# Attention kernel: a hand-made head, a searched instruction order and a 45th key block on VectorE

## The chip, the cores and the metric

The kernel runs on one core of a Trainium2 chip. The time is what the device needs for one execution, in microseconds (us); smaller is better. A single core has no second die to be compared with, so a run counts as fast here unless it is over 1.5% above the fastest one of its kernel. "Span" is the time from the first to the last record in a profile; it is about 1.8 us shorter than the time of the same execution. "Faster" or "slower" is said from 2% on.

## The reference

It is a gated mix of a full 16-head softmax attention and a spectral filter over 2048 positions of 448 features (head size 28), all inputs in bfloat16. Cut to what matters:

```python
def reference(A_x, A_wqkv, A_wo, B_x, B_w_r, B_w_i, gate_w):
    # B, S, D, H = 1, 2048, 448, 16
    g = sigmoid((A_x * gate_w).sum(-1, keepdims=True))
    q, k, v = split(A_x @ A_wqkv)                  # 16 heads of 28
    p = softmax(einsum("bhqd,bhkd->bhqk", q, k) * 28 ** -0.5)
    a = merge(einsum("bhqk,bhkd->bhqd", p, v)) @ A_wo
    b = irfft2(rfft2(B_x) * (B_w_r + 1j * B_w_i))  # ... cut
    return g * a + (1 - g) * b
```

The 2048 x 2048 scores of 16 heads need 67 million exponentials. They are the bulk of the work.

## The kernel before

Queries are handled in 16 groups (four heads times 512 queries), keys in 16 blocks of 128. A block of a group is four units of 128 x 512 scores. ScalarE takes units three at a time from the PSUM tile `psA` and two at a time from `psB`, in alternation, and writes the exponentials into a ring of 28 slots, from which TensorE multiplies them with the values. `ND` says how many key blocks of each group go to VectorE instead, which approximates the exponential by integer arithmetic on the bits in four phases:

```python
    ND = [1, 2, 3, 3, 2, 3, 3, 3, 3, 3, 3, 3, 3, 3, 3, 3]   # 44 of 256 blocks on VectorE
    # ... cut
            # ScalarE: one step of the row of exponentials
            def fe(st=st, slot=slot, u0=u0):
                self.pin(nc.scalar.activation(out=self.ring[:, u0:u0 + len(st), :], in_=slot[:, 0:len(st), :],
                                              func=ACT.Exp, scale=LN2 / UNITS))
    # ... cut
                # VectorE: from PSUM (four times for a block), then one of four phases in SBUF
                def f1(s=s, it=it, ys=ys):
                    self.pin(nc.vector.tensor_scalar(out=ys[:, s, :], in0=self.bgi(it), scalar1=127 * UNITS,
                                                     scalar2=0.0, op0=ALU.add, op1=ALU.max))
                # ... cut
                def g1(ys=ys, pds=pds, f=f):
                    fl = lambda t: t[:].rearrange("p a b -> p (a b)")
                    self.pin(nc.vector.tensor_scalar(out=fl(pds).bitcast(U16), in0=fl(ys), scalar1=float(PHASE[f]),
                                                     scalar2=0.25, op0=ALU.add, op1=ALU.mult))
```

The head loads weights and the first 512 rows of x, pads the weights, transposes x on TensorE, and computes the first q and k. Fourteen matmuls on zeros ("warm-ups") are there to get TensorE to its fast rate. In the traces here matmuls of 256 columns stand 0.11 us apart at the fast rate and 0.21 at the half rate:

```python
        d1 = [self.dma(free_dims(self.U[:], [[112, 3], [1, 112]], W0 + 336 * i), ...,     # 84 KB of k or q weights
                       eng=eng, dur=0.55, lat=2.9) for i, eng in ((0, "SP"), (1, "AQ"))]
        d2 = self.dma(free_dims(self.U[0:64, 0, :], [[112, 2], [1, 112]], W0 + 672), ..., # 28 KB, 64 rows, q and k
                      eng="AQ", dur=0.55, lat=2.9)
        # ... cut
        self.wready["k", 0] = padcopy("k", 0, raw0("k"), dk, K0 + 3.95, "DVE")
        self.wready["q", 0] = padcopy("q", 0, raw0("q"), dq, K0 + 4.05, "ACT")
        for i in range(14):
            self.pe(256, lambda: self.mm(self.psA[:, 2, 0:256], self.zero[:, 0:P], self.zero[:], True, True),
                    (ms["zero"],), K0 + i * .01, dur=0.214)
```

All 3,123 operations are made first and then emitted in an order that is written out as a list. `FILLS` adds matmuls on zeros at places where TensorE would sit idle, and `BANKS` chooses one of two PSUM banks for each short-lived tile.

```python
        done = set()
        for p, i in enumerate(ORDER):
            while j < len(FILLS) and FILLS[j][0] == p:
                n, t = FILLS[j][1:]
                # ... cut: append a filler matmul of n columns
            o = self.ops[i]
            assert all(d in done for d in o.deps)
            done.add(o)
            order.append(o)
        return order
```

The waits on the chip come from the tiles that the instructions read and write, not from the `deps` of this list; the list only fixes each engine's order.

## Time and profile before

| | before |
|---|---|
| time, median of 3 runs (range) | 411.84 us (410.68 to 412.26) |
| span of the profiled run | 409.6 us |
| head: start to first exponential | 13.72 us |
| row: first exponential's start to the last one's end | 386.81 us |
| tail: from there to the end of the span | 9.07 us |
| exponentials on ScalarE | 340 |

Three rows sum up to the span, and every change must show in one of them. In a line of the page the figures behind the bar are busy time in us and mean ns of one instruction, then the idle time of the engine ahead of the group and what ended most of it. In a timeline the first two columns are start and duration in us; `x4` is four instructions in a row, and the bracket gives the idle time ahead and what ended it. The prediction shows the lines.

### The profile page before, as it was taken

What the parts mean: (1) busy time and instruction counts of PE and PEld (TensorE: products, weight loads), DVE (VectorE), ACT (ScalarE), POOL (GpSimd) and SP (SyncE); (2) the same over time, 40 slices, a digit from 0 to 9 for tenths busy, and PEclk for the clock granted to TensorE, in tenths of its full rate; (3) what the DMA queues carried; (4) which work ended last, traced back from release to release, by engine and by line L of the source; (5) the groups of instructions that cost most, each with busy time, mean ns of one, the idle gap of its engine ahead of it and who ended that gap; (6) DMA issues with size and microseconds to landing.
All of it is one profiled execution on the core that took longest, in us unless ns stands there. A gap on an engine that the chain in (4) does not pass through costs nothing.

```text
span 409.6 us, 12755 instructions
## 1 busy us (share of the span) xinstructions
PE 392.5 (96%) x5469; PEld 152.3 (37%) x5469; DVE 365.9 (89%) x629; ACT 389.8 (95%) x358; POOL 41.9 (10%) x95
## 2 busy tenths in 40 slices
PE   5999999999999999999999999999999999999995
PEld 4644333333543333334333333433334343333333
DVE  2768998889999999999999999999999998988784
ACT  2699999999999999999999999999999999999991
POOL 6121400000040000000040000001400000000000
PEclk9999999999999999999999999999999999999999
DMA  7820000000221221101110010043121110010111
GB/s 200 240 51 5 3 3 2 4 2 4 74 52 46 56 63 43 44 3 47 44 45 3 2 29 21 19 123 107 44 71 55 30 28 14 2 37 2 27 52 63
DMA packets 26548, 18.00 MB, mean 44 GB/s; under 512 B 10704, under 2 KB 24956, under 8 KB 26492
## 3 DMA queue, kind: packets, MB, share of 16 engines
q1 hardware_dynamic: 25660, 16.94, 15.3%
q8 instruction: 42, 0.69, 0.7%
q10 hardware_dynamic: 832, 0.26, 0.3%
q14 instruction: 14, 0.11, 0.1%
HBM read 11.31 MB, written 1.84 MB: 32 GB/s over the span
## 4 chain that ended last, share of the span: by engine, by line
ACT 53%; PE 34%; issue 8%; DVE 2%; POOL 1%; DMA 1%; ACTq 0%; DVEq 0%; POOLq 0%
ACT ring L1286 53%; PE bg L572 14%; PE pvb L572 9%; PE psA L572 6%; PE psB L572 5%; DVE y L1239 1%; DMA CR<-cRB 1%; PE bg L581 0%; POOL wpq L671 0%; POOL vd L875 0%; POOL wo L880 0%; DVE pd L1249 0%; ACT w L1068 0%; ACT t L1498 0%; DVE pvs L1399 0%
## 5 line engine op out<-in xcount | busy, mean ns | idle before, releaser
L1286 ACT ACTIVATE ring<-psA 128x1536 bf16<-128x1536 f32 x170 | 266.1, 1566 | 2.7 <-PE psB L572 1.9
L1286 ACT ACTIVATE ring<-psB 128x1024 bf16<-128x1024 f32 (+1 forms) x170 | 193.2, 1136 | 0.6 <-PE psB L572 0.6
L1239 DVE TENSOR_SCALAR y<-bg 128x512 uint16<-128x512 f32 x176 | 117.8, 683 | 8.2 <-PE bg L572 6.8
L1249 DVE TENSOR_SCALAR pd<-y 128x2048 uint16<-128x2048 uint16 x176 | 117.5, 685 | 0.6
L572 PEld LDWEIGHTS <-k 32*128 32x128 bf16 (+1 forms) x1064 | 44.0, 91 | 116.9 <-issue 110.3
L572 PE MATMUL pvb<-ring,vw 128*32 128x512 bf16 (+1 forms) x872 | 75.4, 377 | 0.3 <-DVE pvs L1399 0.2
L572 PE MATMUL psA<-q,k 32*128 32x512 bf16 (+1 forms) x525 | 68.0, 376 | 5.1 <-ACT ring L1286 2.8
L572 PE MATMUL psB<-q,k 32*128 32x512 bf16 (+1 forms) x347 | 67.8, 378 | 0.8 <-ACT ring L1286 0.5
L572 PE MATMUL bg<-q,k 32*128 32x512 bf16 x176 | 65.7, 380 | 0.8 <-DVE y L1239 0.3
L572 PE MATMUL pvb<-pd,vd 128*32 128x512 bf16 x704 | 63.2, 384 | 0.0
L572 PEld LDWEIGHTS <-vw 128*32 128x32 bf16 x872 | 20.7, 95 | 29.6 <-issue 24.6
L572 PEld LDWEIGHTS <-vd 128*32 128x32 bf16 x704 | 16.7, 94 | 27.6 <-issue 23.8
L1404 POOL CAST rhl<-rr 128x16 bf16<-128x16 f32 x15 | 4.0, 267 | 223.9 <-DVE rr L1403 223.9
L572 PEld LDWEIGHTS <-xT 128*128 128x128 bf16 (+3 forms) x512 | 19.3, 96 | 12.7 <-issue 10.1
L1142 POOL TENSOR_SCALAR vd<-vf 128x348 bf16<-128x348 f32 x16 | 19.5, 1222 | 33.4 <-DVE vf L1131 32.6
L1624 DVE CAST Y<-bg 128x450 bf16<-128x450 f32 x32 | 19.7, 618 | 1.2 <-PE bg L572 0.7
L572 PE MATMUL bg<-xT,wpk 128*32 128x512 bf16 (+2 forms) x244 | 18.3, 381 | 0.0
L572 PE MATMUL bg<-xT,wpq 128*32 128x512 bf16 (+1 forms) x240 | 17.7, 383 | 0.0
L572 PE MATMUL bg<-Bd,xT 128*32 128x450 bf16 (+1 forms) x256 | 17.1, 357 | 0.0
L572 PE MATMUL bg<-wo,q 128*32 128x448 bf16 x236 | 16.7, 355 | 0.0
L572 PE MATMUL bg<-Bd,xtok 113*32 113x448 bf16 x240 | 16.5, 355 | 0.0
L572 PE MATMUL bg<-X,R 128*32 128x225 bf16 (+1 forms) x288 | 14.3, 294 | 0.0
(130 smaller groups left out, 322.6 us busy)
## 6 DMA issues: line engine op xcount, KB each, us to landing
U<-Y SPq DMA_DIRECT2D x32, 112.5 KB
CR<-cRB SPq DMA_DIRECT2D x8, 256.0 KB
out_dram<-U SPq DMA_DIRECT2D x14, 112.0 KB
CR<-cCS SPq DMA_DIRECT2D x8, 192.0 KB
xtok<-in_A_x_dram SPq DMA_DIRECT2D x3, 448.0 KB
xT<-escr SPq DMA_DIRECT2D x2, 512.0 KB
Wg<-in_B_w_r_dram SPq DMA_DIRECT2D x8, 112.5 KB
Wg<-in_B_w_i_dram SPq DMA_DIRECT2D x8, 112.5 KB
```

The lines of the kernel that those rows point to most:

```text
L572: self.pin(self.nc.tensor.matmul(out, lhsT=lhsT, rhs=rhs, start=start, stop=stop, **kw))
L1142: self.pin(nc.gpsimd.tensor_scalar(out=self.vd[g][:, f, :, :, 0:DH + 1], in0=self.vf[:], scalar1=PHGAIN[f], scalar2=None, op0=ALU.mult))
L1239: self.pin(nc.vector.tensor_scalar(out=ys[:, s, :], in0=self.bgi(it), scalar1=127 * UNITS, scalar2=0.0, op0=ALU.add, op1=ALU.max))
L1249: self.pin(nc.vector.tensor_scalar(out=fl(pds).bitcast(U16), in0=fl(ys), scalar1=float(PHASE[f]), scalar2=0.25, op0=ALU.add, op1=ALU.mult))
L1286: self.pin(nc.scalar.activation(out=self.ring[:, u0:u0 + len(st), :], in_=slot[:, 0:len(st), :], func=ACT.Exp, scale=LN2 / UNITS))
L1404: b = self.pool(0.3, lambda: self.pin(nc.gpsimd.tensor_copy(out=rhl[:, 0, :], in_=rr[:])), (a,), kk)
L1624: self.pin(nc.vector.tensor_copy(out=y[:], in_=self.bgi(it)[:, 0:F2]))
```

## The change

The intent is to start the exponentials sooner by a head arranged by hand, to give one more key block to VectorE, and to have everything else ordered by a search. In code it is one number and three lists (and `TA`, which only feeds sort keys that the written-out order overrides):

```diff
@@ class Sched / lists @@
-ORDER = ( 119, 1, 0, 2, 7, 3, 12, 22, 94, 4, 21, 13, 32, 6, ...   # 3,123 numbers, cut
+ORDER = ( 1, 2, 7, 0, 8, 10, 19, 3, 20, 21, 12, 11, 13, 4, ...    # 3,134 numbers, cut
-FILLS = ( (117, 192, 0), (126, 256, 1), (144, 256, 0), ...         # 10,976 columns in all, cut
+FILLS = ( (121, 256, 0), (121, 256, 0), (121, 256, 0), ...         # 12,640 columns in all, cut
-BANKS = ( ... cut
+BANKS = ( ... cut
-TA, TB = 43.678, 14.609
+TA, TB = 36.0, 14.609
@@ class Kernel @@
-    ND = [1, 2, 3, 3, 2, 3, 3, 3, 3, 3, 3, 3, 3, 3, 3, 3]
+    ND = [1, 3, 3, 3, 2, 3, 3, 3, 3, 3, 3, 3, 3, 3, 3, 3]
```

## The prediction

> **What bounds the kernel now.** I read the page first (busy shares, chain, groups), then the timelines of ScalarE, VectorE and TensorE over the first 20 us, the waits, and the busy time by stretches.
>
> ```profile
> PE 392.5 (96%) x5469; PEld 152.3 (37%) x5469; DVE 365.9 (89%) x629; ACT 389.8 (95%) x358; POOL 41.9 (10%) x95
> ...
> ACT 53%; PE 34%; issue 8%; DVE 2%; POOL 1%; DMA 1%; ACTq 0%; DVEq 0%; POOLq 0%
> ...
> L1286 ACT ACTIVATE ring<-psA 128x1536 bf16<-128x1536 f32 x170 | 266.1, 1566 | 2.7 <-PE psB L572 1.9
> L1286 ACT ACTIVATE ring<-psB 128x1024 bf16<-128x1024 f32 (+1 forms) x170 | 193.2, 1136 | 0.6 <-PE psB L572 0.6
> L1239 DVE TENSOR_SCALAR y<-bg 128x512 uint16<-128x512 f32 x176 | 117.8, 683 | 8.2 <-PE bg L572 6.8
> L1249 DVE TENSOR_SCALAR pd<-y 128x2048 uint16<-128x2048 uint16 x176 | 117.5, 685 | 0.6
> ```
>
> Three engines look full, but ScalarE leads: 340 exponentials (170 of three units of 512 columns, 170 of two) wait only 3.3 us together (2.7 + 0.6), and more than half of the chain is that one line. So the end is: start of the first exponential, plus the row of exponentials, plus a tail. The start and the tail:
>
> ```profile
> 4.40 0.66 DVE L688 COPY wpk<-U 128x336 bf16<-128x336 bf16 x1 [4.40 <-DMA U<-in_A_wqkv_dram]
> ...
> 6.69 0.18 DVE L691 COPY wpk<-U 64x112 bf16<-64x112 bf16 x1 [1.31 <-DMA U<-in_A_wqkv_dram]
> ...
> 11.10 0.47 ACT L801 ACTIVATE k<-pvb,cst 128x256 bf16<-128x256 f32 x1 [1.05 <-PE pvb L572]
> ...
> 13.72 1.45 ACT L1286 ACTIVATE ring<-psA 128x1536 bf16<-128x1536 f32 x1 [1.89 <-PE psB L572]
> 15.07 0.59 ACT L1286 ACTIVATE ring<-psB 128x512 bf16<-128x512 f32 x1
> 16.04 1.45 ACT L1286 ACTIVATE ring<-psA 128x1536 bf16<-128x1536 f32 x1 [0.38 <-PE psA L572]
> ...
> 399.83 0.70 ACT L1286 ACTIVATE ring<-psB 128x512 bf16<-128x512 f32 x1
> 405.75 0.63 ACT L1498 ACTIVATE t<-psA,gs 128x448 bf16<-128x448 f32 x1 [5.22 <-PE psA L572]
> ```
>
> Head: 0 to 13.72. Row: 13.72 to about 400.5, that is 386.8 us. Tail: 9.1 us to the span of 409.6. The profiler's duration overlaps the next instruction, so I take start to start from the timeline: the median is 1.33 us after a psA exponential and 0.91 after a psB one (0.48 estimated for a one-unit one). Without any wait the row would take 170 x 1.33 + 168 x 0.91 + 2 x 0.48 = 380.0, so 6.8 us are lost in it: 0.7 in eight small exponentials between, the rest in waits and jitter, none over 1 us.
>
> [...]
>
> ```profile
> 1.55 1.68 PE L572 MATMUL psA<-zero 128*128 128x256 bf16 x7 [1.55 <-POOL zero L664]
> ...
> 7.65 1.06 PE L572 MATMUL psA<-xT,wpk 128*128 128x256 bf16 x4
> ...
> 14.09 0.60 PE L572 MATMUL bg<-xT,wpk 128*128 128x256 bf16 x4
> ```
>
> Four matmuls of 256 columns take 1.06 us with the last one's 0.42 in it, so 0.21 apart; at 14.09 it is 0.60 with 0.27, so 0.11 apart. The whole head was computed at half speed: 7 warm-up matmuls, a gap from 5.4 to 7.5 us, and the fast state only near 12.5. (The page's clock row says 9 in all slices[...].) [...]the 28 KB of weights with 64 rows, third on ScalarE's queue and issued by 2.4 us, landed only at 6.6, although the 84 KB before them had landed at 4.4; a 448 KB load of x issued on the other queue at 1.72 ran beside them.
>
> **The change part by part.** Beside the order, the filler list and the PSUM bank choice, one constant matters: the second group of 512 queries gives 3 instead of 2 key blocks to VectorE (44 to 45 in all). The other changed constant only feeds sort keys which the written-out order overrides.
>
> (a) The 45th block. The built order shows 338 exponentials for 340: one of 1536 and one of 512 columns go. ScalarE saves 1.33 + 0.48 = 1.81 us, on the path. VectorE gains four conversions from PSUM and four phases in SBUF: 4 x 0.683 + 4 x 0.685 = 5.5 us, beside other work. TensorE gains 12 value matmuls (four phases for one), in 3 column-tiled groups of 0.22 (pvb starts in the trace), 0.65 us; the four score matmuls are now issued singly, 4 x 0.22 for 1.6 groups of 0.23, another 0.5. The order has 680 changes between row, column and full tiling for 692, and fillers grow from 10,976 to 12,640 columns, +0.7 us[...], placed where idle time was expected. TensorE is about even.
>
> The block falls where VectorE is not idle much:
>
> ```profile
> 13.72:41.00 27.28, 26.89 (x364) 13.09 (x361) 19.99 (x37) 26.56 (x28) 5.38 (x18) 1.00 0.31 80
> 41.00:65.00 24.00, 23.40 (x312) 8.26 (x308) 23.07 (x41) 23.67 (x22) 5.67 (x7) 1.00 0.02 3
> ```
>
> The columns after the length are busy TensorE, its weight loads, VectorE, ScalarE, POOL. Here 27.3 - 20.0 = 7.3 us are free on VectorE before 41 us and 0.9 after; the new order has to pull work into the first stretch. Two memsets that stood there or in the head (0.91 each) now come first of all.
>
> (b) The first loads. In the new order the x load of 448 KB third on the SP queue is replaced by the 117 KB of constants and the 224 KB of x which the head needs; all 448 KB loads come later. Some 360 KB less (448 less 84 for a value weight load moved up) compete. At the 300 to 370 GB/s that the DMA view shows from 5.5 us on, this is 1.0 to 1.2 us. So the 64-row weights should land near 5.5 (5.0 to 6.2) instead of 6.6.
>
> (c) The head. Before, 7.03 us pass from that landing (6.69) to the first exponential. In the new order the 14 warm-up matmuls all come first: 14 x 0.21 = 3 us from about 1.1, then eight transposes to about 5.1.[...] From the landing L, with durations of the trace: weights copied by ScalarE (0.25 + 0.40), its x copy 0.36, so the third q matmul goes at L + 1.0; k, the last q and the second k set, 9 x 0.11, by L + 2.1; eight transposes to L + 2.6; meanwhile the squares; correction matmul, ScalarE's k 0.47 by L + 3.4; VectorE's x copy (0.56) then q's add (0.42) by L + 3.8; scores, first exponential L + 4.2. Unlike before, the q correction no longer stands behind ten transposes and a filler. If the array is still at half speed, the same count gives about L + 5.8.[...] first exponential at 10.5, 3.2 us earlier.
>
> (d) The next steps. Steps three and four wait for the second half of q and k. The same VectorE chain stands there as before (two scalings, two squares, two adds, two x copies), so I expect 0.8 to 1.2 us of wait, against 0.9 now. I take 0.2 off.
>
> (e) The tail is the same list of operations in nearly the same order: 9.1 us.
>
> (f) The searched order. It can win back or lose part of the 6.8 us; both kernels have such an order, and I see nothing that says which is better: 0, give or take 1.5.
>
> Sum: -1.8 (a) - 3.2 (c, with b) + 0.2 (d) = -4.8. From the median 411.84: 407.0 us.
>
> **The rivals.**
> 1. *TensorE is the real bound.* It is busy 328 of 335.5 us between 65 and 400 us, and every change of tiling mode costs it a little (at 200 us a column group starts 0.30 after a row group, for 0.22 within one kind). Then removing ScalarE work is given back as waits before the exponentials, and only the head counts: 411.84 - 3.0 = 408.8. For it: 96% busy, "issue" 8% in the chain. Against it: its busy time uses modelled ends (0.38 us for matmuls that start 0.22 apart), the order has fillers, and the exponentials wait so little.
> 2. *The head gains little.* The landing is set by the latency of small weight rows and not by x, or the array stays slow: first exponential at 12.0 to 12.5, so 411.84 - 1.8 - 1.5 = 408.5. For it: the same queue also carries two wqkv loads with rows of 224 B, during which the DMA view shows only 120 to 190 GB/s. Against it: even then the q correction no longer stands behind ten transposes.
> 3. *VectorE becomes the bound in the first third.* 5.5 us more where 8.2 are free to 65 us; if the exponential pieces on VectorE arrive late, TensorE's value matmuls wait and the ring of exponentials fills: 1 to 3 us lost, 408 to 410. The page's 6.8 us of VectorE waiting for the bg buffers shows that its free time is not all usable.
> 4. *The search found more.* If the new order halves the loss in the row, 3 us more: 404.
>
> **Range and chances.** Centre 407.0; uncertain by 1 us in the head, 1.5 in the order, 0.8 in the block, and by about 0.8 between runs (before: 410.68 to 412.26). Together about 2, so 8 in 10 lie within 404.5 to 409.7. Faster by over 2% needs below 403.6, where rival 4 and the full head must meet: 0.06. Slower by over 2% needs above 420: 0.01. Within 2%: 0.93.
>
> **What would show it.** (a) 338 exponentials, the row 385 us or less from first start to last end; if it stays at 386.8, rival 1 holds. (b) The 64-row copies start before 6.2 us. (c) The first exponential starts between 9.7 and 11.5, and the first projections stand 0.11 us apart and not 0.21. (d) Under 1.3 us of waits before the first five exponentials. (e) Tail 9.1 within 0.3. The prediction is wrong if the first exponential starts after 12 us or if exponentials wait over 6 us in all.

What no trace and no run shows is cut from it, as marked; the three lines behind the first cut are from the timeline of TensorE of the kernel before. The cut in (c) took two terms of the sum with it, allowances of 0.4 us each that were guesses and not worked out from the trace: with them the first exponential came to 5.5 + 4.2 + 0.8 = 10.5 us, 3.2 us earlier, and the whole sum to -4.8 us, that is 407.0 us. Its 0.48 us for an exponential of one unit is an estimate from the two medians of the trace (one unit less takes 1.33 - 0.91 = 0.42 us less), and so is the 0.7 us for the fillers: 1,664 columns more, at 256 in 0.11 us.

## The result, and the profile after

| | before | after | predicted |
|---|---|---|---|
| time, median of 4 runs | 411.36 us | 406.14 us (405.93 to 408.0) | 407.0 |
| span | 409.6 | 404.4 | |
| 64-row k weights copied at | 6.69 | 5.65 | 5.5 (5.0 to 6.2) |
| head: first exponential at | 13.72 | 9.76 | 10.5 (9.7 to 11.5) |
| row | 386.81 | 386.25 | 385 or less |
| of it lost before the first five exponentials | 0.88 | 0.95 | under 1.3 |
| of it lost before the sixth and seventh | 0 | 0.93 | no term for it |
| tail | 9.07 | 8.39 | 9.1 within 0.3 |
| exponentials | 340 | 338 | 338 |

The ratio of the times is 0.9882, with a 95% interval from 0.9845 to 0.9918: within 2%, as predicted. A ratio is the mean time of one kernel's fast runs over the mean of the other's fast runs of the same rounds, so it is not quite the ratio of the medians quoted. "Lost" is start to start less the row's median (1.33 us behind a `psA` exponential, 0.91 behind a `psB` one, both unchanged), counted where it is over 0.12; a small exponential that stands between two counts as a step of its own.

The page of the changed kernel, for the lines of the page shown in the prediction:

```profile
PE 387.8 (96%) x5509; PEld 151.2 (37%) x5509; DVE 370.1 (92%) x637; ACT 388.3 (96%) x356; POOL 43.8 (11%) x95
...
ACT 48%; PE 39%; issue 8%; DVE 3%; DMA 1%; ACTq 0%; DVEq 0%
...
L1287 ACT ACTIVATE ring<-psA 128x1536 bf16<-128x1536 f32 x169 | 263.0, 1556 | 2.5 <-PE psA L573 1.5
L1287 ACT ACTIVATE ring<-psB 128x1024 bf16<-128x1024 f32 (+1 forms) x169 | 191.0, 1130 | 0.5 <-PE psB L573 0.3
```

There are 169 and 169 exponentials for 170 and 170, and VectorE is busier by 4.2 us. But ScalarE's share of the chain fell from 53% to 48% and TensorE's rose from 34% to 39%: by this page TensorE is closer behind.

The timeline of ScalarE, for the head, the start of the row and the tail:

```profile
5.61 0.28 ACT L692 COPY wpq<-U 64x112 bf16<-64x112 bf16 x1 [1.64 <-DMA U<-in_A_wqkv_dram]
...
9.76 1.45 ACT L1287 ACTIVATE ring<-psA 128x1536 bf16<-128x1536 f32 x1 [0.42 <-PE psB L573]
11.10 0.59 ACT L1287 ACTIVATE ring<-psB 128x512 bf16<-128x512 f32 x1
12.30 1.45 ACT L1287 ACTIVATE ring<-psA 128x1536 bf16<-128x1536 f32 x1 [0.60 <-PE psA L573]
...
16.58 1.02 ACT L1287 ACTIVATE ring<-psB 128x1024 bf16<-128x1024 f32 x1 [0.17 <-PE psB L573]
18.14 1.45 ACT L1287 ACTIVATE ring<-psA 128x1536 bf16<-128x1536 f32 x1 [0.54 <-PE psA L573]
...
394.96 1.05 ACT L1287 ACTIVATE ring<-psB 128x1024 bf16<-128x1024 f32 x1
401.01 0.63 ACT L1499 ACTIVATE t<-psA,gs 128x448 bf16<-128x448 f32 x1 [5.00 <-PE psA L573]
```

The first exponential comes 3.96 us sooner, but the second one is followed after 1.20 us (12.30 less 11.10; before, 0.97), and behind the one at 16.58 another 0.65 us are lost. The last exponential ends at 396.01.

The timeline of TensorE, same kernel:

```profile
1.09 3.17 PE L573 MATMUL psA<-zero 128*128 128x256 bf16 x14 [1.09 <-POOL zero L665]
...
6.42 0.49 PE L573 MATMUL psB<-xT,wpq 128*128 128x256 bf16 x3 [1.60 <-ACT wpq L689]
6.74 0.60 PE L573 MATMUL psA<-xT,wpk 128*128 128x256 bf16 x4
```

Four projections take 0.60 us for 1.06 before: 0.11 apart, the fast rate. All 14 warm-ups now stand in one piece ahead of everything. That mends something else too. In the kernel before, three of them stood behind the first exponentials, and two of these fell between scores and the exponential that reads them. The first of the two, in the timeline of TensorE of the kernel before:

```profile
15.39 0.39 PE L572 MATMUL psA<-q,k 32*128 32x256 bf16 x6
15.72 0.28 PE L572 MATMUL psA<-zero 128*128 128x256 bf16 x1
```

The exponential of these scores starts at 16.04, as the prediction's lines show, so 256 columns of its third unit were zeros by then. The other one ran at 27.44 us, behind scores at 27.11 and ahead of their exponential at 27.82. The result stayed within the tolerance, and no run here measured how far it was off.

The span fell by 5.2 us: 3.96 in the head, 0.56 in the row and 0.68 in the tail. The head beat the prediction by 0.7 us and the row missed it by 1.2.

### The profile page after: what moved, and what is told of

Read it like the earlier page. It is cut to its first block, busy times and chain, and to the rows that moved or that the text cites. A ratio compares the mean times of both kernels' runs of the same rounds, so it can differ in the third digit from the quotient of the medians.

```text
span 404.4 us, 12832 instructions
## 1 busy us (share of the span) xinstructions
PE 387.8 (96%) x5509; PEld 151.2 (37%) x5509; DVE 370.1 (92%) x637; ACT 388.3 (96%) x356; POOL 43.8 (11%) x95
## 4 chain that ended last, share of the span: by engine, by line
ACT 48%; PE 39%; issue 8%; DVE 3%; DMA 1%; ACTq 0%; DVEq 0%
ACT ring L1287 47%; PE bg L573 16%; PE pvb L573 11%; PE psA L573 6%; PE psB L573 5%; DMA U<-in_A_wqkv_dram 1%; DVE y L1240 1%; DVE Y L1625 0%; DVE pd L1250 0%; DVE k L995 0%; PE bg L582 0%; ACTq L553 0%; DVE X L1670 0%; ACT w L1069 0%; ACT t L1499 0%
## 5 line engine op out<-in xcount | busy, mean ns | idle before, releaser
L1287 ACT ACTIVATE ring<-psA 128x1536 bf16<-128x1536 f32 x169 | 263.0, 1556 | 2.5 <-PE psA L573 1.5
L1287 ACT ACTIVATE ring<-psB 128x1024 bf16<-128x1024 f32 (+1 forms) x169 | 191.0, 1130 | 0.5 <-PE psB L573 0.3
L1240 DVE TENSOR_SCALAR y<-bg 128x512 uint16<-128x512 f32 x180 | 120.6, 683 | 5.4 <-PE bg L573 3.8
L1250 DVE TENSOR_SCALAR pd<-y 128x2048 uint16<-128x2048 uint16 x180 | 120.4, 688 | 0.4
L573 PEld LDWEIGHTS <-k 32*128 32x128 bf16 (+1 forms) x1064 | 42.7, 91 | 121.0 <-issue 115.1
L573 PE MATMUL psA<-q,k 32*128 32x512 bf16 (+1 forms) x522 | 66.8, 376 | 4.9 <-ACT ring L1287 3.8
L573 PEld LDWEIGHTS <-xT 128*32 128x32 bf16 (+3 forms) x512 | 19.0, 96 | 11.3 <-issue 8.8
L1143 POOL TENSOR_SCALAR vd<-vf 128x348 bf16<-128x348 f32 x16 | 20.4, 1272 | 22.2 <-DMA k<-nrow 13.3
```

Of the source, the lines that this page charges most:

```text
L573: self.pin(self.nc.tensor.matmul(out, lhsT=lhsT, rhs=rhs, start=start, stop=stop, **kw))
L1143: self.pin(nc.gpsimd.tensor_scalar(out=self.vd[g][:, f, :, :, 0:DH + 1], in0=self.vf[:], scalar1=PHGAIN[f], scalar2=None, op0=ALU.mult))
```

## The experiments

Twelve kernels ran, the last two kernels on another chip than the ten before them, each with runs of the kernel before on the same chip; its median was 410.6 to 411.3 us. All results were within the tolerance.

### The changed kernel again

No edit; it is the yardstick for the others.

> The changed kernel once more, for the spread of its executions. Theory: the ratio comes again at 0.988 (0.985 to 0.991), nearly all executions at 405.9 to 406.3 us; where the half-speed state of TensorE lasts through the head[...], an execution is 1.5 to 2 us longer, as the one at 408.0 was: about one in four or five. Rival: that one was plain noise, and the executions spread evenly over 405.5 to 408.

The median was 407.56 us (406.24 to 408.14), ratio 0.9899 (0.9857 to 0.994). In the profile the first exponential started at 9.89 and the row took 386.27 us. So the row of 386.3 is no accident. Two runs lie at 406.2 to 406.5 and four at 407.5 to 408.1; in the first measurement it was three to one. "Nearly all" at 406 was wrong, and a third set of runs of this kernel (below, under the memsets) also has 406.80 and 407.01. So 16 runs do not show two groups, and do not decide between theory and rival.

### Only the head changed

The list of the kernel before, with the changed kernel's order up to exponential step 6; 44 blocks.

```diff
-ORDER = before's
+ORDER = after's up to the seventh exponential, then before's for all that is left
     ND = [1, 2, 3, 3, ...]
```

> The kernel before (44 blocks) with the new order, warm-ups, loads and fillers of all that precedes the seventh exponential, and its own order for the rest. Theory (the row of exponentials sets the end, so that the head goes to the end one to one): first exponential at 9.8 us instead of 13.7, and 4.0 us less in all, some 407.4, ratio 0.990. Rival (TensorE is the bound, the rest waits for it or for the loads): first exponential at 9.8 all the same, but 2 us or less in all, since the waits come later.

The median was 408.66 us, ratio 0.9929 (0.9879 to 0.9978). The first exponential started at 9.79, so the head's gain is whole, but the row grew from 386.81 to 387.91 us: 0.71, 0.24, 0.28 and 0.65 us are lost in its first seven steps, for 0.49 and 0.39 before. In time that is 2.5 us less, between the theory's 4.0 and the rival's 2. Set against the changed kernel's 386.25, the block and the searched order together then bring 1.66 us. The row did not swallow the block; the new head's start-up waits hid it.

### Only the head undone

The reverse: the changed kernel with the kernel before's head, 45 blocks.

```diff
+ORDER = before's up to the seventh exponential, then after's for all that is left
     ND = [1, 3, 3, 3, ...]
```

> The changed kernel (45 blocks, its own order) with the old order, warm-ups, loads and fillers of all that precedes the seventh exponential. Theory: first exponential at 13.7, the time 4.0 us over the changed kernel, some 410.1, ratio 0.997. Rival: the new rest needs the early loads of the new head, and waits for them: 411.5 or more.

The median was 410.88 us (408.93 to 412.49), ratio 0.9984 (0.9929 to 1.0039): joined in this way, nothing is left that can be measured. The time is near the theory's 410.1, but not for its reason. Its profiled run was the quickest one, and its head was not what it had been in the kernel before. The timeline of ScalarE:

```profile
6.25 0.28 ACT L667 COPY wpq<-U 64x112 bf16<-64x112 bf16 x1 [2.27 <-DMA U<-in_A_wqkv_dram]
...
11.22 1.45 ACT L1262 ACTIVATE ring<-psA 128x1536 bf16<-128x1536 f32 x1 [1.44 <-PE psB L548]
```

From the copy to the first exponential it is 4.97 us, against 6.97 in the kernel before (6.75 to 13.72) with the same order: here the projections stood 0.11 us apart. The same head runs at either rate. The join also cost: 0.8, 1.14 and 0.99 us are lost at 17.5, 19.2 and 21.7 us (until 20.75 TensorE stands idle for 1.22 us ahead of two warm-ups that the old list leaves over for the join), so its row of 387.49 us says nothing clean about the block.

### The block undone

The changed kernel with 44 blocks again; the two steps that come back were put in by hand, the fillers kept.

```diff
-    ND = [1, 3, 3, 3, ...]
+    ND = [1, 2, 3, 3, ...]
+ORDER = after's, with two steps of exponentials put in behind group 1's others
```

> The changed kernel with 44 blocks: the one block goes back to ScalarE, its two exponentials stand at its place and all else keeps its order. Theory A (ScalarE's row sets the end): 1.8 us over the changed kernel, 407.9, ratio 0.9925. Theory B (the trace after shows the row only 0.6 us shorter: TensorE or VectorE gives the rest back): 0.3 to 0.8 over it, 406.4 to 406.9, ratio 0.989 to 0.990.

The median was 429.77 us, ratio 1.0404 (granted clock 0.972 in the profile): neither theory. The timeline of TensorE shows where it began:

```profile
64.06 0.39 PE L548 MATMUL psB<-q,k 32*128 32x512 bf16 x2 [0.47 <-ACT ring L1262]
65.40 0.60 PE L548 MATMUL psA<-q,k 32*128 32x512 bf16 x3 [0.95 <-ACT ring L1262]
```

TensorE waited 0.47 and 0.95 us for ScalarE, and from then until 88.7 us, with breaks, matmuls of 512 columns take 0.60 us for 0.39. The view of stretches shows this as a granted clock of one half (the third column from the end):

```profile
66.00:75.00 9.00, 8.84 (x66) 1.86 (x65) 3.01 (x5) 4.09 (x5) 0.68 (x2) 0.50 0.00 0
```

(In the head of the kernel before, from 7.5 to 12.5 us, that column says 1.00 although the spacing is doubled there too, 0.21 us: it showed the fall here, and not the slow start there.) At the half rate TensorE cannot keep up: five exponentials wait 1.4 to 3.6 us each, 11 us in all, which is about half of what the row grew by. It became 409.06 us. As a test of the block it failed. It shows that the half rate in the row is dear. That the holes brought it is likely but not shown: idle stretches of the same length were followed by no fall elsewhere (1.10 us at 147.8 in the memset kernel, 0.95 at 150.9 with the load in front, 0.94 and 1.00 at 103.6 and 116.9 in this one).

### One block more: 46

The changed kernel with `ND[4]` = 3, placed by hand like its neighbours, fillers kept.

```diff
-    ND = [1, 3, 3, 3, 2, 3, ...]
+    ND = [1, 3, 3, 3, 3, 3, ...]
```

> The changed kernel with one key block more on VectorE (the fifth query group takes 3 instead of 2: 46 in all, 336 or 337 exponentials for 338), placed by hand among the same operations of the neighbouring groups. Theory A (ScalarE's row is the bound and a block is worth its exponentials, start to start 1.33 + 0.48 or 1.33 + 0.91): 1.3 to 2.2 us faster, 404.3 to 405.5. Rival B (TensorE, 96% busy, is as near the bound, so a block's exponentials come back as waits): within 0.6 us of the changed kernel, 405.8 to 407. Rival C (the hand placement opens holes in TensorE where the array falls to half speed, as in the run with the block undone): over 410.

The median was 431.57 us, ratio 1.0463: the third case of the expectation. From 134 to 142 us TensorE waits 0.5 to 0.9 us at a time for VectorE, and from 143 to 166 us its matmuls of 512 columns take 0.60 us, at a granted clock of 0.50: the same fall, in which 14 us are lost. (This profile also has a half-rate head, first exponential at 12.28.) VectorE is busy 19.5 of 20 us between 120 and 140 us in the changed kernel already, so there was hardly room for another 5.5 us. What a 46th block would be worth under an order made for it stays open.

### Without warm-ups

The changed kernel with the warm-ups 8 columns wide instead of 256.

```diff
-self.mm(self.psA[:, 2, 0:256], self.zero[:, 0:P], self.zero[:], True, True)
+self.mm(self.psA[:, 2, 0:8], self.zero[:, 0:P], self.zero[:, 0:8], True, True)
```

> The changed kernel with its 14 warm-up matmuls shrunk from 256 to 8 columns: nothing else differs. Theory A (the earlier first exponential is half load and half clock[...]): the first projections stand 0.21 us apart and not 0.11, the first exponential starts 1.2 to 2.0 us later (11.1 to 11.8 for 9.8), and the waits in the next six exponentials do not shrink by as much, so 407.2 to 408.5 us. Rival B (warm-up does not matter, only the order of the loads and of the head): projections still 0.11 apart or first exponential within 0.4 us of 9.8, 406.0 to 407.0.

The median was 408.55 us (407.92 to 408.87), ratio 0.9932 (0.9875 to 0.999). The timeline of TensorE:

```profile
6.83 1.06 PE L548 MATMUL psA<-xT,wpk 128*128 128x256 bf16 x4
```

The projections stand 0.21 us apart, the first exponential starts at 11.54 for 9.76, and the row (386.09) is as it was. Theory A: the warm-ups earn 1.8 us in the profile, and all four runs now lie in the slower half of the changed kernel's or above it, so this is more than the chance of one profile.

### The 448 KB load back in front

The changed kernel with one 448 KB load of x third on the SP queue again, ahead of the constants.

```diff
 SP queue: x 224 KB, q weights 84 KB,
+          x 448 KB,
           constants 117 KB, x 224 KB, ...
```

> The changed kernel with one 448 KB load of x put back as the third transfer of the SP queue, ahead of the constants and the last 224 KB of the head's x, as the kernel before has it. Theory A (the small 64-row weights land late because a big load competes[...], and the head's own loads stand behind it): the copies of the 64-row weights start at 6.4 to 6.9 instead of 5.6, the constants and x land about 1 us later too, and the first exponential starts 0.8 to 1.5 us later, at 10.6 to 11.3; 407.0 to 408.0. Rival B (latency of many short rows decides, not the competing bytes): the copies start within 0.3 us of 5.6 and the first exponential within 0.4 of 9.8.

The median was 409.94 us, ratio 0.9955 (0.9904 to 1.0007). The timeline of ScalarE:

```profile
6.76 0.28 ACT L667 COPY wpq<-U 64x112 bf16<-64x112 bf16 x1 [2.80 <-DMA U<-in_A_wqkv_dram]
...
12.87 1.45 ACT L1262 ACTIVATE ring<-psA 128x1536 bf16<-128x1536 f32 x1 [0.74 <-PE psB L548]
```

The small weights land 1.15 us later than in the changed kernel, as A has it: the 448 KB load ahead delays them. The first exponential moved by more than A's 0.8 to 1.5, by 3.11 us, because this head ran at the half rate as well. From the copy on it takes the same time as without warm-ups, 6.11 us. Whether the longer pause of TensorE (2.45 us ahead of the projections) brought the half rate, one profile cannot tell.

### Only the load moved, in the kernel before

```diff
 SP queue: x 224 KB, q weights 84 KB,
-          x 448 KB,
           constants, x, ...
+          x 448 KB,
```

> The kernel before with one change: the 448 KB load of x that was third on the SP queue is issued after the constants and the head's other x loads. Theory A: the 64-row weights land about 1 us earlier (copies at 5.5 to 5.9 for 6.69), the first exponential moves by 0.7 to 1.2 us if the head's TensorE order does not eat it (12.5 to 13.0 for 13.72); 410.0 to 411.0. Rival B (the loads by themselves bring nothing, because the old order of the head, its second bank and the half-speed array set the first exponential): landing earlier but first exponential within 0.4 us of 13.7 when the array is at half speed; 411 to 412.

The median was 410.14 us (409.31 to 413.73), ratio 0.9985 (0.9927 to 1.0044). The small weights were copied at 5.59 for 6.75 us, and the first exponential started at 11.81: 1.91 sooner, more than the landing, because the array became fast near 9.4 us instead of near 12.5. The landing is as A said. The profiled run is the longest of the four: after TensorE had waited 1.25 us for VectorE at 278 us, its matmuls ran at the half rate until 285.9 (granted clock 0.51), and 3.9 us were lost there. The other three runs took 409.31 to 410.54 us at a clock of 0.998 to 1.000, so a fall can also happen in single executions of one and the same list.

### ScalarE made lighter

The changed kernel, wrong on purpose though it stayed within the tolerance: ten exponentials of 1024 columns do only 512.

```diff
-            def fe(st=st, slot=slot, u0=u0):
-                self.pin(nc.scalar.activation(out=self.ring[:, u0:u0 + len(st), :], in_=slot[:, 0:len(st), :],
+            def fe(st=st, slot=slot, u0=u0, i=i):
+                w = 256 if i in range(41, 331, 32) else 512
+                self.pin(nc.scalar.activation(out=self.ring[:, u0:u0 + len(st), 0:w], in_=slot[:, 0:len(st), 0:w],
```

> The changed kernel, wrong on purpose: ten two-unit exponentials, spread evenly from step 41 to step 329, do 512 of their 1024 columns and leave the rest of their ring slots as they were. Nothing changes for TensorE, VectorE or the transfers. That takes about 0.43 us from ScalarE ten times (0.91 start to start less 0.48). Theory A (ScalarE's row alone sets the pace from 10 to 396 us, and TensorE and VectorE have room): the row shortens by 3.5 to 4.3 us, 401.8 to 402.8. Rival B (TensorE, 96% busy, or VectorE, is as near the bound, so that less ScalarE work comes back as waits before exponentials): the row shortens by under 1.5 us, 404.8 to 406.2. In between: a part of it is given back, and the share says how much a further block could be worth.

The median was 408.47 us (406.83 to 408.74), ratio 0.9945: not faster than the changed kernel. In the profile the row is 384.59 us, so 1.66 of the 4.3 us arrived. The timeline of ScalarE at the first of the ten, and the scores that TensorE makes for the exponential behind it:

```profile
59.35 1.53 ACT L1288 ACTIVATE ring<-psA 128x1536 bf16<-128x1536 f32 x1
60.69 0.69 ACT L1288 ACTIVATE ring<-psB 128x512 bf16<-128x512 f32 x1
61.46 1.45 ACT L1288 ACTIVATE ring<-psA 128x1536 bf16<-128x1536 f32 x1
```

```profile
60.94 0.42 PE L573 MATMUL psA<-q,k 32*128 32x512 bf16 x3
```

The next exponential starts 0.77 us later and not the estimated 0.48: its scores were not there yet. TensorE could not make them sooner. They go to `psA`, which the exponential from 59.35 on reads until 60.88; they start 0.05 us later, and the exponential 0.50 to 0.52 behind them. Over the ten such places 3.65 us are given back, and 1.0 is gained elsewhere. Worked out from the trace, this turn of `psA` (0.05 and 0.495 us at its shortest) accounts for 2.6 of the 3.65; only about 0.9 comes from TensorE starting later than the turn allows. So the figure lies between the theories, but it does not measure how near TensorE is to the bound: a step of one unit is shorter than the turn of the other buffer, and the experiment mostly found that. The time says less than the row, because this profiled run was also one with a half-rate head (first exponential at 11.96, at 9.76 in the changed kernel, by the same head), and the other three had granted clocks of 0.992 to 0.998 over the whole run. The timelines of VectorE and GpSimd in this profile show a second thing:

```profile
5.07 2.47 DVE L689 COPY wpk<-U 128x336 bf16<-128x336 bf16 x1
```

```profile
4.34 1.70 POOL L881 MEMSET wo<- 128x448 bf16 x4
...
6.91 0.53 POOL L672 MEMSET wpk<- 128x512 bf16 x1
```

VectorE's copy of the k weights, 0.25 to 0.78 us where it is short, takes 2.47 us here and ends at 7.54, just behind GpSimd's unbroken run of memsets (7.44). The same figure, 2.46 or 2.47, stands in the profiles of the 46-block kernel and of the next experiment; in none of the other profiles with this head. In three of those the copy starts within 0.01 us of the same moment (5.06 or 5.07) and takes 0.25, 0.26 and 0.66 us. So the memsets may have held it up. The reverse fits too: in the profiles with this head where the copy is short, the four memsets of `wo` take 1.80 us and more, and in the three with the long one 1.70. (In the changed kernel it is the fourth that lasts 0.57 us for 0.47.) But it is argued from coincidence and not shown: no experiment separates it.

### The small weights on the other queue

The changed kernel with the 28 KB third on the SP queue, and ScalarE's copy of the 128-row q weights put first.

```diff
-                      eng="AQ", dur=0.55, lat=2.9)      # 28 KB of 64-row weights
+                      eng="SP", dur=0.55, lat=2.9)
```

> A try at beating both kernels: the changed kernel with the 28 KB of 64-row weights moved from ScalarE's queue to the SP queue, third, right behind the q weights, and ScalarE's copy of the 128-row q weights put ahead of the 64-row one. Theory A (in the changed head the landing of the 64-row weights at 5.6 us is still what the first projections wait for): 64-row copies at 4.6 to 5.2, first projection at 5.7 to 6.1 for 6.42, first exponential 0.3 to 0.8 us earlier than 9.8, 405.3 to 405.9. Rival B (the constants and the second 224 KB of x, now issued 0.5 us later, become the wait, or the 64-row landing does not move): first exponential within 0.2 us of 9.8 or later, 406 to 407.

The median was 408.98 us (408.34 to 410.03), ratio 0.9958 (0.9935 to 0.9981): not as good as the changed kernel's (0.9882 to 0.9899 in its three sets). The landing did what A says: ScalarE's 64-row copy started at 4.80. The timeline of TensorE shows what became of it:

```profile
5.20 0.51 PE L548 MATMUL psB<-xT,wpq 128*128 128x256 bf16 x3
7.59 0.61 PE L548 MATMUL psA<-xT,wpk 128*128 128x256 bf16 x4 [1.88 <-DVE wpk L664]
...
9.34 0.42 PE L548 MATMUL pvb<-sq,cst 128*128 128x256 bf16 x1
```

The q projections went at 5.20, 1.2 us sooner than in the changed kernel. The k projections had to wait for VectorE's copy, which took 2.47 us, and during the next transposes TensorE fell back to the half rate: 0.42 us for a matmul that took 0.27 in the changed kernel, with a granted clock of 0.50 from 9 to 12 us. All six runs have a mean granted clock of 0.991 to 0.996, so none seems free of it. The first exponential came at 11.28. That is B's "or later", but by another cause than B's. It points to a better edit: keep this landing, and take the copy off VectorE.

### GpSimd's memsets told to wait: no effect

```diff
-self.pool(0.5, lambda g=g: self.pin(nc.gpsimd.memset(self.wo_pad[g][:], 0.0)), (), 100 + g)
+self.pool(0.5, lambda g=g: self.pin(nc.gpsimd.memset(self.wo_pad[g][:], 0.0)), self.wready["k", 0][1:], 100 + g)
```

> The changed kernel with one more dependency: GpSimd's run of memsets (the four of wo at 4.34 us and the six behind them, until 8.4 us) waits for VectorE's copy of the 64-row k weights. In three of the ten profiled runs with this head, VectorE's copy of the 128-row k weights took 2.47 us instead of 0.25 to 0.76 and ended just when the unbroken run of memsets ended. Theory A[...]: the copy takes under 0.8 us in the profile, the slower of the two groups of times (407.5 to 408.1 us of the changed kernel) gets rarer; what is left of it comes from the half-speed head alone: median 405.9 to 406.6 and none above 408. Rival B (the 2.47 us have another cause, such as the landing of the weights): some runs above 407.9 stay, and the profile may show a long copy again without memsets beside it.

The median was 407.19 us (405.94 to 408.39), ratio 0.9897. The edit did nothing: the dependency is one of the list only, and no wait came of it; the profile has the first of these memsets at 4.33 us still, and the copy it should have waited for at 5.65. So the theory was not tested, whether the memsets hold the copy up stays open, and this is a third set of runs of the changed kernel (first exponential 9.82, copy 0.66 us). The 16 runs of the three sets, on different chips, lie between 405.93 and 408.39, median 407.2.

### A head put together from the findings

The last kernel takes the landing of the small weights on the SP queue, has ScalarE instead of VectorE copy the 128-row k weights, and puts three more warm-ups into the gap behind the first transposes. (The memsets' dependency is in it too, without effect.)

```diff
-                      eng="AQ", dur=0.55, lat=2.9)      # 28 KB of 64-row weights
+                      eng="SP", dur=0.55, lat=2.9)
-        self.wready["k", 0] = padcopy("k", 0, raw0("k"), dk, K0 + 3.95, "DVE")
+        self.wready["k", 0] = padcopy("k", 0, raw0("k"), dk, K0 + 3.95, "DVE", "ACT")   # 128 rows by ACT, 64 by DVE
-        for i in range(14):
+        for i in range(17):                              # the last three behind the transposes in ORDER
```

> A second try at beating both kernels, from what the runs showed: the 28 KB of 64-row weights third on the SP queue (they landed at 4.8 us there), ScalarE and not VectorE copies the 128-row k weights, GpSimd's run of memsets waits for VectorE's 64-row k copy, and three more warm-up matmuls stand in the gap behind the transposes of x. Theory A (the head is set by the landing and the copies, and the array keeps the fast state over the shorter gap): first projection at 5.2 to 5.7 for 6.42, first exponential at 8.5 to 9.2 for 9.76 in the fast state, the row within 0.5 us of 386.3, 404.8 to 405.7 us. Rival B (the second 224 KB of x or the constants, issued later, become the wait): first exponential 9.4 to 10.0, 405.8 to 406.5. Rival C (the array is at half speed all the same): first exponential about 10.3, 406.5 to 407.2.

The median was 405.33 us, ratio 0.9855 (0.9827 to 0.9882), against 0.9897 for the changed kernel. It is the fastest kernel, and its five runs lie between 405.3 and 405.76. The timelines of TensorE and ScalarE:

```profile
4.90 0.52 PE L548 MATMUL psA<-zero 128*128 128x256 bf16 x3
...
5.95 0.60 PE L548 MATMUL psA<-xT,wpk 128*128 128x256 bf16 x4
```

```profile
8.96 1.45 ACT L1265 ACTIVATE ring<-psA 128x1536 bf16<-128x1536 f32 x1 [0.42 <-PE psB L548]
```

The first exponential starts at 8.96, 0.8 us sooner, at the fast rate, and the row is 386.13 us. That is theory A. The spread of 2.5 us of the changed kernel is gone. Which of the three edits removed it, the faster rate kept through the gap or the copy moved off VectorE, was not tried apart.

## Why the prediction was right or wrong

The class and the time were right (407.0 against 406.14, within the range). Step by step:

**(a) The 45th block, -1.8: nearly right.** The row shrank by only 0.56, but by 1.66 when the head is the same (head-only kernel against the changed one). That sum holds the searched order too; the two attempts to move a block alone ended in the half rate, so the block's own share is open. Rival 1, TensorE as the bound, is not the whole truth, or nothing would have come. How much of it holds stays open: TensorE's share of the chain rose, but the test with lighter exponentials measured mostly the turn of `psA`.

**(b) The landing, 5.5: right** (5.65), and the load of 448 KB is the cause: put back, it costs 1.15 us; moved away in the kernel before, it gains 1.16.

**(c) The head: right in mechanism, 0.7 better than said.** The profiles allow a split. From ScalarE's copy of the 64-row weights to the first exponential it is nearly the same time for a given order and rate, wherever VectorE's copy is not held up (6.19 and 6.66 us in the two profiles with this head where it is):

| kernel | copy at | first exponential | between | rate |
|---|---|---|---|---|
| before | 6.75 | 13.72 | 6.97 | half |
| old head in the changed kernel | 6.25 | 11.22 | 4.97 | fast |
| changed | 5.61 | 9.76 | 4.15 | fast |
| changed, again | 5.75 | 9.89 | 4.14 | fast |
| head only | 5.65 | 9.79 | 4.14 | fast |
| without warm-ups | 5.43 | 11.54 | 6.11 | half |
| 448 KB back in front | 6.76 | 12.87 | 6.11 | half |

So of the 3.96 us, the landing gave 1.14 (6.75 to 5.61), the order of the head 0.86 (6.97 less 6.11, at the half rate; at the fast rate 4.97 less 4.15 = 0.82), and the rate 1.96 (6.11 less 4.15). The estimate had 4.2 us from the landing on, plus the two allowances of 0.4; at the fast rate neither was needed (4.15). Of the seven profiles with this head unaltered (the changed kernel, its two repeats, head only, block undone, 46 blocks, lighter ScalarE) five had the fast rate and two the half rate: this head, too, runs at either. The two with the half rate are also the two with VectorE's long copy. The copy's delay did not make them slow, as their first three q projections took 0.80 us for 0.49 before the copy had ended; why the two come together is open. The old head was seen at both rates too, so the 1.96 is the difference of two profiles and no fixed gain of the change. That the rate explains the spread of the changed kernel's times is not shown: no run above 406.8 us was profiled.

**(d) The start-up waits, +0.2: the step that failed.** It is +1.0: 1.88 us are lost in the first seven steps for 0.88. The waits that were forecast, at steps three and four for the second half of q and k, came as said: 0.95 us for 0.88. The sum had no term for steps six and seven, which lose 0.28 and 0.65 and lost nothing before. The seventh exponential is the first that needs the second block of 512 keys. VectorE's last instruction on these keys, in the kernel before and in the changed one:

```profile
18.99 0.69 DVE L994 TENSOR_TENSOR k<-k,bg 128x512 bf16<-128x512 bf16 x1 [0.50 <-PE bg L572]
```

```profile
16.92 0.69 DVE L995 TENSOR_TENSOR k<-k,bg 128x512 bf16<-128x512 bf16 x1
```

It ends at 17.61, 2.07 us sooner, while the first exponential comes 3.96 sooner; the scores start at 17.70 and the exponential at 18.14. I took the chain of VectorE to be the same and so the wait to be the same. But the new head makes the first exponential sooner than what comes behind it: VectorE's first scaling of the second half of q stood 0.55 us ahead of the first exponential before (13.17) and stands 0.44 behind it now, as it waits for TensorE until 10.20. That the loss belongs to this order of the head, not to the block, is shown by the head-only kernel; and most of it moves along when the head is late (0.81, 0.22, 0.24, 0.28 and 0.66 us without warm-ups).

**(e) The tail, 9.1 within 0.3: wrong by 0.4.** It is 8.39. ScalarE's last instruction starts 5.00 us behind the last exponential for 5.22, and the last output lands sooner after it. The two joined kernels tell where it comes from: with the list of the kernel before behind the seventh exponential the tail is 9.24 (head only), with the list of the changed kernel it is 8.42 (old head). So it belongs to the rest of the list with its banks and fillers, not to the head; no run took it further apart.

**(f) The searched order, 0 within 1.5.** Nothing contradicts it: the row is 8.0 us above its minimum in the changed kernel and 7.8 in the head-only one, so the search neither won nor lost in the row; what it may have won in the tail is in (e). (The minimum of the changed kernel is 169 x 1.33 + 167 x 0.91 + 0.48 for the small exponential + 1.05 for the last one = 378.3 us.) Rival 4 did not happen.

The sum was right partly because two errors offset each other: 0.7 gained in the head and 0.7 in the tail, against 0.8 in (d) and some tenths in (a). Rival 2 fell with the first exponential at 9.76. Rival 3 found no trace in the early stretch, but the 46-block kernel shows what it looks like where VectorE has no room.

## What to carry to other kernels

Take a row that sets the end apart into head, row and tail, and in the head look for one event (here a landing of 28 KB) from which everything else is a fixed distance. Expect that starting such a row sooner exposes the next producer, and count the waits of its first steps again. Where TensorE is nearly full, a fall to half its clock cost 4 to 14 us here; it came behind holes of 0.5 to 1.3 us in the lists that were patched by hand, though not behind every such hole: keep TensorE fed in the head and in the row, and do not put in work by hand without moving the fillers as well. And before you shorten one step of a row, look when the buffer of the next step comes free: a step shorter than that turn gained nothing more here (0.77 us from start to start, for an estimated 0.48).
